# Loading part of w2 as two transfers, for 119 and for 9 partitions, in a one-token attention and gated feed-forward kernel

## The chip, the cores and the metric

The kernel runs on one core of a Trainium2 chip. The metric is device time in microseconds for one execution, here the median of several. A core has a matrix engine (TensorE, PE in the profile, with its weight loads as PEld), VectorE (DVE), ScalarE (ACT), GpSimd (POOL) and SyncE (SP), which here only issues transfers. Sixteen DMA engines move data between the device memory and the on-chip memory of 128 partitions.

## The reference, cut to what matters

One token is decoded. An attention over a cache of 32,768 positions with 32 query heads on 8 key/value heads, and a gated feed-forward branch, are mixed by a gate.

```python
q = (x @ wq).reshape(...)                     # x: (1, 1, 512), wq: (512, 4096)
scores = einsum("bhqd,bhkd->bhqk", q, k) * Dh ** -0.5
o = softmax(scores) @ v                       # k_cache, v_cache: (1, 8, 32768, 128)
a = o.reshape(...) @ wo                       # wo: (4096, 512)
gate = einsum("bsd,df->bsf", x, w1)           # w1, w3: (512, 1792)
up = einsum("bsd,df->bsf", x, w3)
b = einsum("bsf,fd->bsd", silu(gate) * up, w2)  # w2: (1792, 512)
g = sigmoid((x * gate_w).sum(-1))
out = g * a + (1 - g) * b
```

All of it is float32.

## The kernel before

The caches are cut into 32 units, four for each of the eight key/value heads. A unit is one block of keys (k0 to k31) and one of values (v0 to v31), each a transfer of 4 MB in which every partition receives 32 KB. All large loads go through `load` (line 69 issues them) on SyncE's queue and land in a pool named `stream` with four buffers, so a load can be issued as soon as the buffer four loads earlier has been read to its end.

The main loop runs over `UNITS + LAG` steps with `LAG = 5`: step i loads k of unit i and v of unit i - 5, transposes the keys on DVE in four chunks and multiplies them by the queries (lines 181 and 188), and multiplies the probabilities of an earlier unit by its values (`values`, line 277). The softmax of a head, and what follows its values, is cut into small steps which `defer` puts into a list and `tick` runs a fixed number of ticks later; this fixes the order of the instructions on each engine by hand. The feed-forward's w1 and w3 come in steps 2 and 3, and the hidden row is spread over partitions early (`htp`). In the last five steps no keys are left; v27 to v31 are loaded and used.

After the loop stands what the change touches. w2 (1792 x 512) is held as 14 row blocks: partition p has the rows 14p to 14p + 13, 2 KB each, 28 KB contiguous in device memory. The tile `w2t` (line 392) takes the stream buffer that v28 had, so its transfers (line 395) are issued when v28's matmuls are done. Three transfers bring blocks 0 to 7, 8 to 11 and 12 to 13, each for all 128 partitions. They stand in SyncE's queue behind v29, wo of the last head, v30 and v31. The last thing SyncE issues is the output (line 415).

On PE the order after the matmuls of v31 (line 277, tile o) is: heads of the last unit (po, line 289, which waits for ACT's copy ob, line 283), the first eight blocks of w2 (`ff_down(0, 8)`, tile pb, line 401, four matmuls a block), the product with wo (pa, line 303), the other six blocks of w2. DVE then adds pa to `acc`, scales it by the gate, and combines it with pb into `res` (line 414), which goes out.

Of the kernel before, what the change touches and what calls it, by code (L numbers as in the profile page):

```python
# [14 lines left out]
P = 128  # L15
# [4 lines left out]
def kernel(  # L20
# [13 lines left out]
    nc = tc.nc  # L34
# [29 lines left out]
    def misc(name):  # L64
        return ps_m.tile([P, 512], F32, tag="misc", name=name)
# [325 lines left out]

    w2t = stream.tile([P, FR, D], F32, tag="stream", name="w2")
    w2d = w2.rearrange("(p k) e -> p k e", k=FR)
    for a, b in ((0, 8), (8, 12), (12, 14)):
        nc.sync.dma_start(w2t[:, a:b, :], w2d[:, a:b, :])
    pb = misc("pb")

    def ff_down(a, b):
# [45 lines left out]
```

## Time and profile before

| | us |
|---|---|
| median of 3 runs | 705.38 (705.27 to 705.67) |
| the profiled execution | 705.64 |
| its span, first to last instruction | 703.9 |
| PE busy | 449.4 (64%) |
| PE weight loads busy | 161.6 (23%) |
| DVE busy | 317.6 (45%) |
| ACT busy | 69.3 (10%) |
| TensorE clock granted, mean | 0.735 |
| moved by DMA | 296.65 MB, mean 421 GB/s |

The span is what the profiler sees from the first to the last instruction of one execution; the time of that execution is 1.7 us longer. All numbers in the views come from this one execution. A view of lines or groups gives busy time and the mean of one instruction; the chain that ended last is followed back from the last instruction, each time to what released it. In the views of stretches, each engine has its busy time and its count of instructions in brackets, then come the clock granted to TensorE as a share of the full one, the mean busy share of the 16 DMA engines, and what they moved. A transfer's time "to landing" runs from its issue to the moment when its last part has arrived; a transfer that waits in the queue behind others has that wait in it.

### The profile page before, as it was taken

How to read it: one execution, taken by the hardware profiler on the slowest of the kernel's cores; microseconds unless marked ns; L12 is line 12 of the kernel's file. 1: busy time of each engine (PE TensorE's matmuls, PEld its weight loads, DVE VectorE, ACT ScalarE, POOL GpSimd, SP SyncE). 2: the span in 40 equal slices, each digit the busy share in tenths (PEclk: the TensorE clock that was granted, in tenths of full speed). 3: DMA queues.
4: the chain of work that ended last, by engine and by line, in shares of the span. 5: the costliest groups of instructions: out<-in, count | busy, mean ns of one | idle time of the engine just before them, and what ended most of it. 6: DMA issues, size and time to landing. Idle time of an engine off the chain costs nothing.

```text
span 703.9 us, 6780 instructions
## 1 busy us (share of the span) xinstructions
PE 449.4 (64%) x3014; PEld 161.6 (23%) x3014; DVE 317.6 (45%) x237; ACT 69.3 (10%) x175; POOL 1.6 (0%) x12
## 2 busy tenths in 40 slices
PE   2666578776863496545863679535966568547666
PEld 0331143114210042112320143102320142103213
DVE  1079556654752444554642455542643546523000
ACT  0100101210200002000120003000020002000100
POOL 0000000000000000000000000000000000000000
PEclk9766856695676759776676657967596757868868
DMA  8999999999999999999999999999999999999994
GB/s 369 435 435 426 435 429 399 427 429 434 427 426 431 436 427 432 423 427 434 427 428 431 434 426 435 424 428 434 429 433 417 437 426 435 420 436 430 423 428 198
DMA packets 14772, 296.65 MB, mean 421 GB/s; under 512 B 1556, under 2 KB 1560, under 8 KB 5784
## 3 DMA queue, kind: packets, MB, share of 16 engines
q1 hardware_dynamic: 14600, 296.23, 98.5%
q8 instruction: 23, 0.38, 0.2%
q14 instruction: 5, 0.04, 0.0%
q10 hardware_dynamic: 144, 0.00, 0.0%
HBM read 296.23 MB, written 0.00 MB: 421 GB/s over the span
## 4 chain that ended last, share of the span: by engine, by line
DMA 61%; PE 18%; DVE 14%; issue 6%; ACT 0%; SPq 0%; DVEq 0%
DMA k<-in_A_k_cache_dram 48%; DVE kt L181 12%; DMA v<-in_A_v_cache_dram 10%; PE pf L204 7%; PE s L188 4%; DMA wq<-in_A_wq_dram 3%; PE o L277 2%; PE pt L159 2%; DVE mx L213 1%; PE pw L320 1%; PE pq L142 1%; PE ph L350 1%; PE pb L401 0%; DVE rp L154 0%; DVE rep L345 0%
## 5 line engine op out<-in xcount | busy, mean ns | idle before, releaser
L181 DVE STREAM_TRANSPOSE kt<-k 128x2048 f32<-128x2048 f32 x128 | 288.9, 2290 | 225.7 <-DMA k<-in_A_k_cache_dram 219.7
L188 PE MATMUL s<-kt,win 128*32 128x512 f32 x1024 | 201.3, 872 | 209.1 <-DVE kt L181 168.4
L277 PE MATMUL o<-v,prob 128*32 128x512 f32 x1024 | 135.6, 677 | 15.1 <-DMA v<-in_A_v_cache_dram 15.1
L188 PEld LDWEIGHTS s<-kt,win 128*32 128x32 f32 x1024 | 25.7, 128 | 328.3 <-issue 181.0
L195 ACT COPY sb<-s 128x512 f32<-128x512 f32 x32 | 35.4, 1106 | 480.0 <-PE s L188 480.0
L277 PEld LDWEIGHTS o<-v,prob 128*32 128x32 f32 x1024 | 34.3, 124 | 105.3 <-issue 77.6
L204 PEld LDWEIGHTS pf<-pick,sb 128*128 128x128 f32 x256 | 52.5, 313 | 24.1 <-issue 24.1
L204 PE MATMUL pf<-pick,sb 128*128 128x64 f32 x256 | 55.3, 406 | 0.0
L213 DVE TENSOR_REDUCE mx<-pf 128x4 f32<-128x512 f32 x16 | 11.1, 692 | 49.6 <-PE pf L204 49.6
L245 ACT ACTIVATE prob<-pf,nm 128x128 f32<-128x128 f32 x64 | 23.4, 498 | 36.3 <-DVE nm L241 36.3
L296 DVE TENSOR_TENSOR otp<-po,recip 128x4 f32<-128x4 f32 x8 | 1.3, 167 | 51.4 <-PE po L289 51.4
L142 PE MATMUL pq<-wq,xp 128*32 128x512 f32 x64 | 10.6, 824 | 17.9 <-DMA wq<-in_A_wq_dram 17.9
L245 ACT ACTIVATION_READ_ACCUMULATOR prob<-pf,nm 128x1 f32 x64 | 14.8, 232 | 0.0
L154 DVE COPY rp<-qs 128x512 f32<-128x512 f32 x8 | 2.8, 415 | 24.5 <-ACT qs L148 24.5
L159 PE MATMUL pt<-ident,rp 128*128 128x4 f32 x64 | 11.3, 313 | 1.7 <-DVE rp L154 1.7
L159 PEld LDWEIGHTS pt<-ident,rp 128*128 128x128 f32 x64 | 11.2, 275 | 3.5 <-issue 3.5
L283 ACT COPY ob<-o 128x512 f32<-128x512 f32 x8 | 4.7, 587 | 73.5 <-PE o L277 73.5
L303 PE MATMUL pa<-wo,otp 128*32 128x128 f32 x256 | 11.8, 343 | 0.0
L303 PEld LDWEIGHTS pa<-wo,otp 128*32 128x32 f32 x256 | 10.1, 143 | 6.3 <-issue 6.0
L289 PEld LDWEIGHTS po<-fold,ob 128*128 128x128 f32 x64 | 7.7, 191 | 8.3 <-ACT ob L283 8.3
L289 PE MATMUL po<-fold,ob 128*128 128x4 f32 x64 | 8.4, 255 | 1.4 <-ACT ob L283 1.4
L142 PEld LDWEIGHTS pq<-wq,xp 128*32 128x32 f32 x64 | 2.6, 142 | 25.0 <-issue 19.8
(52 smaller groups left out, 71.8 us busy)
## 6 DMA issues: line engine op xcount, KB each, us to landing
k<-in_A_k_cache_dram SPq DMA_DIRECT2D x32, 4096.0 KB, 30.0
v<-in_A_v_cache_dram SPq DMA_DIRECT2D x32, 4096.0 KB, 34.8
wq<-in_A_wq_dram SPq DMA_DIRECT2D x2, 4096.0 KB, 16.9
wo<-in_A_wo_dram SPq DMA_DIRECT2D x8, 1024.0 KB, 27.4
w<-in_B_w_dram SPq DMA_DIRECT2D x2, 3584.0 KB, 33.8
w<-in_B_w_dram SPq DMA_DIRECT2D x1, 2048.0 KB, 30.2
w<-in_B_w_dram SPq DMA_DIRECT2D x1, 1024.0 KB, 32.3
w<-in_B_w_dram SPq DMA_DIRECT2D x1, 512.0 KB, 33.1
```

The lines of the kernel that those rows point to most:

```text
L142: nc.tensor.matmul(pq[b][32 * j:32 * j + 32, :], xp[:, c, :], wq_t[c // 2][:, o:o + REP * DH], start=(c == 0), stop=(c == NC - 1),)
L159: nc.tensor.matmul(pt[:, 4 * a:4 * a + 4], rp[:, a, :], sel, start=True, stop=True)
L181: nc.vector.transpose(kt.rearrange("p (n i) -> p n i", i=32), kin.rearrange("p (n c j) -> p c n j", c=4, j=32)[:, c],)
L188: nc.tensor.matmul(s_ps[0][32 * g:32 * g + 32, :], win[:, h, c, :], kt[:, 512 * g:512 * g + 512], start=(c == 0), stop=(c == 3),)
L195: nc.scalar.copy(sb[h][:, :, :, m], s_ps[0].rearrange("p (n i) -> p n i", i=32))
L204: nc.tensor.matmul(pf[h, f][:, 64 * a:64 * a + 64], sb[h][:, 8 * f + a].rearrange("p i m -> p (i m)"), pick, start=True, stop=True,)
L213: nc.vector.tensor_reduce(mx[:, f, :], pf[h, f].rearrange("p (n q) -> p q n", q=REP), axis=AX.X, op=ALU.max)
L245: nc.scalar.activation(prob[h % 2][:, 0:1024].rearrange("p (a n q) -> p a n q", a=16, q=REP)[:, :, 8 * f:8 * f + 8, q], pf[h, f].rearrange ...
L277: nc.tensor.matmul(o_ps[0][32 * t:32 * t + 32, :], prob[h % 2][:, o:o + 32], vt[:, n * P:(n + 4) * P], start=(r == 0 and g == 0), stop=(r ...
L289: nc.tensor.matmul(po[:, 0:REP], ob[:, b * P:(b + 1) * P], fold[:, 4 * b:4 * b + 4], start=(b == 0), stop=(b == 3),)
L303: nc.tensor.matmul(pa[32 * j:32 * j + 32, 0:P], otp[h % 2][:, q, :], wo_t[h][:, q, j * P:(j + 1) * P], start=(q == 0), stop=(q == REP - 1),)
L320: nc.tensor.matmul(p[32 * j:32 * j + 32, 0:FJ], xp[:, c, :], ff[name][:, o:o + FJ], start=(c == 0), stop=(c == NC - 1),)
```

## The change

The transfer of blocks 0 to 7 is cut. Blocks 0 to 2 are loaded by two transfers, one for partitions 0 to 118 and one for partitions 119 to 127; blocks 3 to 7 have a transfer of their own for all partitions. The two later transfers, the bytes moved and the matmuls stay as they are.

```diff
     w2t = stream.tile([P, FR, D], F32, tag="stream", name="w2")
     w2d = w2.rearrange("(p k) e -> p k e", k=FR)
-    for a, b in ((0, 8), (8, 12), (12, 14)):
-        nc.sync.dma_start(w2t[:, a:b, :], w2d[:, a:b, :])
+    for a, b, p0, p1 in ((0, 3, 0, 119), (0, 3, 119, P), (3, 8, 0, P), (8, 12, 0, P), (12, 14, 0, P)):
+        nc.sync.dma_start(w2t[p0:p1, a:b, :], w2d[p0:p1, a:b, :])
     pb = misc("pb")
```

## The prediction

> **What bounds the kernel now.** I read the page first.
>
> ```profile
> span 703.9 us, 6780 instructions
> DMA  8999999999999999999999999999999999999994
> DMA 61%; PE 18%; DVE 14%; issue 6%; ACT 0%; SPq 0%; DVEq 0%
> ```
>
> The DMA engines are over 90% busy in nearly every slice and hold 61% of the chain that ended last: the kernel streams its caches. The diff touches only its last transfer, so the chain after 640 us comes next, in order of time (start, duration, what).
>
> ```profile
> 653.61 36.15 DMA v<-in_A_v_cache_dram
> 689.77 0.04 issue
> 689.81 5.15 PE o L277 x32
> 694.96 0.02 issue
> 694.98 0.59 ACT ob L283
> 695.57 0.04 issue
> 695.62 1.05 PE po L289 x8
> 696.67 1.88 PE pb L401 x64
> 698.56 0.87 PE pa L303 x32
> 699.43 1.35 PE pb L401 x48
> 700.78 0.03 issue
> 700.81 0.35 DVE res L414
> ```
>
> The last block of values, v31, lands at 689.77. Behind it PE, ACT and DVE need eleven microseconds. w2 stands nowhere on this chain: both pb pieces follow PE's own earlier work. When does w2 land? The issues of its three transfers, then the page's times from issue to landing:
>
> ```profile
> 664.43 1.28 SPq L395 DMA_DIRECT2D w<-in_B_w_dram  x3
> ...
> L395 SPq DMA_DIRECT2D w<-in_B_w_dram x3: 328/424/425, 664.4 to 665.3; - x3
> ...
> w<-in_B_w_dram SPq DMA_DIRECT2D x1, 2048.0 KB, 30.2
> w<-in_B_w_dram SPq DMA_DIRECT2D x1, 1024.0 KB, 32.3
> w<-in_B_w_dram SPq DMA_DIRECT2D x1, 512.0 KB, 33.1
> ```
>
> Blocks 0 to 7 land at 664.43 + 30.2 = 694.6 and are read from 696.6; blocks 12 and 13 land at 665.3 + 33.1 = 698.4. They are needed after 32 of the 48 matmuls that start at 699.25 (below), about 0.026 us each, so at 700.1. w2 has 1.7 us to spare at its end and 2.0 at its start.
>
> One more view decides the case: the stretches around the end, with PE's busy time, granted clock (PEclk), the DMA share and GB/s at the right.
>
> ```profile
> 691.50:692.50 1.00, 1.00 (x12) 0.32 (x8) 0.00 (x0) 0.00 (x0) 0.00 (x0) 0.50 0.99 410
> 692.50:693.50 1.00, 1.00 (x16) 0.25 (x12) 0.00 (x0) 0.00 (x0) 0.00 (x0) 0.85 0.56 233
> 693.50:694.50 1.00, 1.00 (x16) 0.18 (x8) 0.00 (x0) 0.00 (x0) 0.00 (x0) 1.00 0.57 238
> 694.50:695.50 1.00, 0.40 (x4) 0.00 (x0) 0.00 (x0) 0.52 (x1) 0.00 (x0) 1.00 0.56 233
> 695.50:696.50 1.00, 0.88 (x8) 0.88 (x8) 0.00 (x0) 0.07 (x1) 0.00 (x0) 1.00 0.36 147
> 697.50:698.50 1.00, 1.00 (x47) 1.00 (x43) 0.00 (x0) 0.00 (x0) 0.00 (x0) 1.00 0.08 25
> ```
>
> The share falls in one step, 0.99 to 0.56, and stays there: 0.44 x 16 = 7 engines have run dry at 692.5, nine go on, the last until 698.4. So the sixteen engines are up to six microseconds apart, and what "v31 has landed" means is set by the latest of the nine.
>
> **The change, part by part.** Blocks 0 to 2 (6,144 bytes a partition) leave the first transfer and become two: partitions 0 to 118 and 119 to 127. Blocks 3 to 7 become the third.
>
> *Issue and waits.* Two more issues at 0.33 to 0.43 us each put the last one some 0.9 us later, near 666.2. It is hidden by 24 us of queue in front of w2; without that cover it would cost 0.9. Behind them SyncE has only the output's issue at 701.19. PE gets up to two more waits; the one that shows beside the first pb costs 51 ns, while PE waits for ACT's ob anyway.
>
> ```profile
> L401 PEldq EVENT_SEMAPHORE  x1: 51/51/51, 695.6 to 695.6; - x1
> ```
>
> *Who carries the 119 rows.* No transfer before has a number of rows that sixteen does not divide, except the output's four. A 4 MB block takes 9.74 us between the landings of v30 and v31 (starts 680.07 and 689.81 below), 262,144 bytes an engine, or 26.9 GB/s; one 6,144-byte row is 0.228 us. Bounds: spread over sixteen, 8 rows to an engine at most, 0 us more; all on one engine, 119 x 0.228 = 27.1 us. 119 is 7 x 17, so in equal shares it is seven engines with 17 rows, 3.9 us instead of 1.8; nine rows in equal shares go to nine engines. I take seven: the flat share before 691.5 says that 128 rows are dealt in equal shares, and seven is the most that 119 allows. Those seven then have 18 rows for 8, 2.3 us more; the engines left out have 8 rows, 1.8 us, less.
>
> [...]
>
> *Which seven.* The trace does not name engines. I take it that they are the seven early ones, since all nine late ones form a group apart (0.56, flat for three rows); the other case is a rival. The early seven have 14 blocks, 229,376 bytes, 8.5 us each, so they reach w2 at 692.5 - 8.5 = 684.0. That is 5.8 us before v31 has landed.
>
> *What those rows meet.* [...] Is 26.9 GB/s the engine's limit, or that of the way into its partitions? The rows cannot say: with nine engines and then one or two active the last one still needed 698.4 - 694.6 = 3.8 us for six blocks (98,304 bytes, 26 GB/s), so it is not the sum of all that limits, but it was alone on its partitions. Lower bound, the engine limits: v31 is not delayed, 0 us. Upper bound, the way limits: each gets 119/16 = 7.4 of these rows, at most 8, 1.7 to 1.8 us. If rows share, the seven need up to 2 x 3.9 = 7.8 us, of which 5.8 us, three quarters, come before v31's end: 1.3 us. The rows do not decide between the ends. I take 1.4 us, from the shared case: every rate seen had each engine on partitions of its own, and 26.9 GB/s came out alike in full and in thin traffic, which a narrow way into the partitions explains without more; the other end keeps a chance of its own.
>
> [...]
>
> *What 1.4 us on v31 costs.* Here the clock comes in.
>
> ```profile
> 680.07 6.54 PE L277 MATMUL o<-v,prob 128*32 128x512 f32 x32 [7.03 <-DMA v<-in_A_v_cache_dram]
> 689.81 5.09 PE L277 MATMUL o<-v,prob 128*32 128x512 f32 x32 [3.20 <-DMA v<-in_A_v_cache_dram]
> 699.25 1.49 PE L401 MATMUL pb<-w,htp 128*32 128x128 f32 x48
> ...
> 679.13:682.54 3.41, 2.47 (x12) 0.60 (x16) 0.00 (x0) 0.00 (x0) 0.00 (x0) 0.50 0.96 413
> 682.54:685.96 3.42, 3.42 (x20) 0.79 (x16) 0.00 (x0) 0.00 (x0) 0.00 (x0) 0.50 0.97 417
> 685.96:689.38 3.42, 0.65 (x8) 0.00 (x0) 0.00 (x0) 0.00 (x0) 0.00 (x0) 1.00 0.97 414
> 689.38:692.79 3.41, 2.98 (x16) 0.80 (x20) 0.00 (x0) 0.00 (x0) 0.00 (x0) 0.50 0.91 383
> 692.79:696.20 3.41, 2.69 (x26) 0.94 (x18) 0.00 (x0) 0.59 (x1) 0.00 (x0) 1.00 0.54 223
> ```
>
> The same 32 matmuls took 6.54 us for v30 and 5.09 for v31. At half clock one microsecond does half a microsecond's work: v30 had 5.89 at half and 0.65 at full (3.60 of work), v31 2.98 at half and 2.11 at full (3.60 again). The clock changes on a grid of 3.41 us. A stretch with 2.98 us of matmuls was followed by full clock, one with 2.47 by another half one. If v31 starts at 689.81 + 1.4 = 691.21, only 1.58 us of 689.38 to 692.79 are busy, the half clock lasts to 696.20, and the group ends at 696.20 + 3.60 - (696.20 - 691.21)/2 = 697.30 instead of 694.90: +2.4. For delays of 0.9 and 1.8 us the same line gives 2.15 and 2.6; under about 0.5 us it may stay near 0.2. All that follows, from ob to the output, is shifted by it unchanged.
>
> *Next late?* w2 is not: the seven finish by 684.0 + 7.8 + 0.2 + 11 blocks of 0.61 (6.7) = 698.7, the nine by 689.8 + 1.4 + 0.2 + 6.7 = 698.1, both before 700.1 + 2.4.
>
> **Sum:** issue 0, waits under 0.1, taken as 0, matmuls of v31 +2.4. The profiled execution would go from 705.64 (703.9 of span and 1.7 around it) to 708.0; it lies 0.26 above the median, so 705.38 + 2.4 = 707.8 us.
>
> **Rivals.**
>
> *No shared way* (the other side: not slower). The engines limit, v31 lands as before, the nine finish w2 1.8 us earlier, at 696.6, and nobody had waited: 705.4. For it: the rates fit an engine's limit as well. Against: nothing but the choice of bound above. It decides as soon as v31's delay is zero.
>
> *Shared, but the clock's grid falls otherwise,* or the delay is under 0.5 us: the delay enters alone or halved, +0.2 to +1.3, 706.1.
>
> *Late engines among the seven.* The latest then finishes w2 2.3 us later: 698.4 + 2.3 = 700.7 against 700.1, +0.6 (706.0). With a shared way its 17 rows take up to 3.9 more, 704.6, +4.5 (709.9); I put it at 708.5. The flat 0.56 speaks for a fixed group of nine, but not for which.
>
> *The rows are not bunched:* sixteen carry 7 or 8 rows each, nothing changes, 705.4. Or all 119 on one: 684.0 + 27.1 + 6.9 = 718.0 against 700.1, 723.3.
>
> *Faster.* In unprofiled executions the late engines might lag further and w2 set the end; 1.8 us less on the nine would then give up to -1.8, 703.6. Against: 1.7 us of slack, and 705.64 beside 705.38.
>
> **Chances.** Forecast 0.56; grid or small delay 0.08; no shared way 0.18; late among the seven 0.10 (0.08 of it shared); sixteen 0.03; one 0.02; faster 0.03. A measurement here tells 0.2%, 1.4 us, from no change. Slower: 0.56 + 0.08 + 0.02 = 0.66; within: 0.08 + 0.18 + 0.02 + 0.03 = 0.31; faster 0.03. The range takes in the unchanged time and most of the shared case with late engines: 705.2 to 709.2.
>
> **What would show it.** Right: v31's landing near 691.2 with the same issue time, a half-clock stretch after 692.8, an o group of about 6.1 us, the DMA share still near 1 after 692.5, and no wait of PE for w2. Wrong: v31 at 689.8 again (no sharing), PE waiting for w2 before pb (late engines among the seven), or the first transfer's landing far beyond 700 (one engine).

## The result, and the profile after

The changed kernel takes 711.78 us (median of 4, 711.01 to 712.41) beside 705.52 us (median of 4, 705.27 to 705.89) for the kernel before: a ratio of 1.0087 with a 95% interval of 1.0075 to 1.0100, 6.3 us slower. That is outside the predicted range of 705.2 to 709.2. The sign was right, the size was not.

The page of the changed kernel, from its profiled execution (712.20 us):

```profile
span 710.4 us, 6783 instructions
DMA 62%; PE 17%; DVE 14%; issue 6%; SPq 0%; ACT 0%; DVEq 0%
```

The chain that ended last, after 640 us, in order of time:

```profile
666.89 39.61 DMA w<-in_B_w_dram
706.51 0.04 issue
706.55 0.69 PE pb L401 x16
707.24 0.03 issue
707.26 0.35 DVE res L414
```

Before, this chain ran through v31, its matmuls, ob, po, pb and pa, and w2 stood nowhere on it. Now w2's last transfer stands between its issue at 666.89 and PE's last 16 matmuls, and landed at 706.51; before, it landed at 698.4.

PE's last groups (start, duration, group, in brackets the idle time before them and what ended it):

```profile
679.27 6.06 PE L277 MATMUL o<-v,prob 128*32 128x512 f32 x32 [7.02 <-DMA v<-in_A_v_cache_dram]
692.87 6.09 PE L277 MATMUL o<-v,prob 128*32 128x512 f32 x32 [7.53 <-DMA v<-in_A_v_cache_dram]
700.66 0.86 PE L401 MATMUL pb<-w,htp 128*32 128x128 f32 x24
702.82 1.30 PE L401 MATMUL pb<-w,htp 128*32 128x128 f32 x40 [1.30 <-DMA w<-in_B_w_dram]
705.30 1.08 PE L401 MATMUL pb<-w,htp 128*32 128x128 f32 x32 [0.31 <-DMA w<-in_B_w_dram]
706.55 0.64 PE L401 MATMUL pb<-w,htp 128*32 128x128 f32 x16 [0.17 <-DMA w<-in_B_w_dram]
```

The stream of this execution is 0.80 us ahead of the one before: v30's matmuls start at 679.27 instead of 680.07. From v30 to v31 it then takes 13.60 us instead of 9.74. So v31 is 3.86 us late. Behind it PE waits for w2 three times, 1.30 + 0.31 + 0.17 = 1.78 us, where it never waited before.

The stretches around v31's landing, of before and then of after (DMA share and GB/s at the right):

```profile
684.00:688.00 4.00, 2.61 (x16) 0.40 (x8) 0.00 (x0) 0.00 (x0) 0.00 (x0) 0.75 0.96 410
688.00:692.00 4.00, 2.19 (x12) 0.60 (x16) 0.00 (x0) 0.00 (x0) 0.00 (x0) 0.67 0.98 412
```

```profile
680.00:684.00 4.00, 4.00 (x24) 0.98 (x20) 0.00 (x0) 0.00 (x0) 0.00 (x0) 0.50 0.98 391
684.00:688.00 4.00, 1.33 (x12) 0.12 (x4) 0.00 (x0) 0.00 (x0) 0.00 (x0) 0.93 1.02 244
688.00:692.00 4.00, 0.00 (x0) 0.00 (x0) 0.00 (x0) 0.00 (x0) 0.00 (x0) 0.50 0.89 202
692.00:696.00 4.00, 3.13 (x16) 0.79 (x20) 0.00 (x0) 0.00 (x0) 0.00 (x0) 0.50 0.99 240
```

This is the finding to explain. From 684 on the sixteen engines are as busy as ever (share 0.89 to 1.02) and move little more than half as much. Each packet takes longer: in the trace v31's packets of 32,768 bytes took 1.21 to 1.23 us before, and after the change those that start from 684 on took 1.97 to 2.57 us. So here the busy share does not tell a moving engine from a held one (0.98 with 412 GB/s before, 0.89 with 202 after); only the GB/s beside it does.

The trace also has the completion signals of each transfer, sixteen for 128 rows. I take one signal for one engine's part: before the change seven of the sixteen signals of w2's last transfer came by 693.57 and nine from 695.95 on, and the DMA share from 692.5 to 695.5 is 0.56, nine sixteenths. For v31, us from the span's start:

```text
before  684.16 684.22 684.27 684.44 684.62 684.96 684.97 | 687.35 ... 689.77  (9)
after   684.09 684.12 684.23 684.46 684.59 685.28 685.65 | 689.90 ... 692.82  (9)
```

Seven early and nine late engines, as the falling DMA share had told. The first w2 transfer of the changed kernel has seven signals of its own, at 691.46, 691.63, 692.75, 692.79 and then at 698.71, 698.90 and 699.71; the second has nine. So 119 rows do run on seven engines and nine rows on nine, and three of the seven are late ones. I take it that the same three set w2's end: of the sixteen signals of its last transfer thirteen come by 701.70, and three at 705.78, 705.82 and 706.51, 6.8 to 7.1 us behind those three, where eleven blocks of 0.61 us take 6.7.

### The profile page after: what moved, and what is told of

It is laid out like the page before. It is cut to its first block, busy times and chain, and to the rows that moved or that the text cites. A ratio compares the mean times of both kernels' runs of the same rounds, so it can differ in the third digit from the quotient of the medians.

```text
span 710.4 us, 6783 instructions
## 1 busy us (share of the span) xinstructions
PE 448.0 (63%) x3014; PEld 157.8 (22%) x3014; DVE 317.3 (45%) x237; ACT 69.6 (10%) x175; POOL 1.7 (0%) x12
## 4 chain that ended last, share of the span: by engine, by line
DMA 62%; PE 17%; DVE 14%; issue 6%; SPq 0%; ACT 0%; DVEq 0%
DMA k<-in_A_k_cache_dram 49%; DVE kt L181 12%; PE pf L204 7%; DMA w<-in_B_w_dram 6%; PE s L188 5%; DMA v<-in_A_v_cache_dram 4%; DMA wq<-in_A_wq_dram 3%; PE pt L159 1%; PE o L277 1%; PE pq L142 1%; DVE mx L213 1%; PE ph L350 1%; PE pw L320 1%; DVE rep L345 0%; DVE win L167 0%
## 5 line engine op out<-in xcount | busy, mean ns | idle before, releaser
L277 PE MATMUL o<-v,prob 128*32 128x512 f32 x1024 | 133.2, 667 | 17.9 <-DMA v<-in_A_v_cache_dram 17.9
L142 PE MATMUL pq<-wq,xp 128*32 128x512 f32 x64 | 12.7, 964 | 16.9 <-DMA wq<-in_A_wq_dram 16.9
L303 PE MATMUL pa<-wo,otp 128*32 128x128 f32 x256 | 10.2, 309 | 0.0
L159 PEld LDWEIGHTS pt<-ident,rp 128*128 128x128 f32 x64 | 9.3, 233 | 3.9 <-issue 3.9
L159 PE MATMUL pt<-ident,rp 128*128 128x4 f32 x64 | 9.4, 283 | 1.1 <-DVE rp L154 1.1
## 6 DMA issues: line engine op xcount, KB each, us to landing
v<-in_A_v_cache_dram SPq DMA_DIRECT2D x32, 4096.0 KB, 34.9
```

What stands on the lines that cost most here:

```text
L142: nc.tensor.matmul(pq[b][32 * j:32 * j + 32, :], xp[:, c, :], wq_t[c // 2][:, o:o + REP * DH], start=(c == 0), stop=(c == NC - 1),)
L159: nc.tensor.matmul(pt[:, 4 * a:4 * a + 4], rp[:, a, :], sel, start=True, stop=True)
L277: nc.tensor.matmul(o_ps[0][32 * t:32 * t + 32, :], prob[h % 2][:, o:o + 32], vt[:, n * P:(n + 4) * P], start=(r == 0 and g == 0), stop=(r ...
L303: nc.tensor.matmul(pa[32 * j:32 * j + 32, 0:P], otp[h % 2][:, q, :], wo_t[h][:, q, j * P:(j + 1) * P], start=(q == 0), stop=(q == REP - 1),)
```

## The experiments

Two questions were open: why v31 is 3.9 us late when its own transfer was not touched, and why w2 ends so late. In the table, "v31 late" is the time between the starts of v30's and v31's matmuls less the 9.74 us of before; "v31's packets" is the time of one packet of 32,768 bytes that starts after 685 us; "waits for w2" is PE's idle time ahead of pb. These three come from the profiled execution, the ratio from repeated runs.

| kernel | ratio to before (95%) | v31 late | v31's packets | waits for w2 |
|---|---|---|---|---|
| changed kernel (first blocks, 119 + 9) | 1.0087 (1.0075 to 1.0100) | 3.86 | 2.00 to 2.57 | 1.78 |
| e2, first blocks, all 128 | 0.9993 (0.9983 to 1.0003) | -0.01 | 1.21 to 1.22 | 0 |
| e3, first blocks, 112 + 16 | 1.0052 (1.0037 to 1.0067) | 3.39 | 1.55 to 2.20 | 0 |
| e11, first blocks, 64 + 64 | 1.0059 (1.0043 to 1.0076) | 4.03 | 1.81 to 2.26 | 0 |
| e8, block 0 alone, 119 + 9 | 1.0029 (1.0016 to 1.0042) | 1.64 | 1.45 to 1.84 | 0 |
| e4, last blocks, 119 + 9 | 1.0036 (1.0024 to 1.0049) | -0.01 | 1.21 to 1.22 | 1.59 |
| e7, last blocks, 112 + 16 | 1.0011 (1.0001 to 1.0021) | -0.02 | 1.21 to 1.22 | 1.30 |
| e10, w2 as before, v31 in four parts | 1.0003 (0.9993 to 1.0014) | | | 2.15 |

**e2, the cut without uneven partitions.** In the diffs of e2, e3 and e4 a minus marks the line of the changed kernel.

```diff
-    for a, b, p0, p1 in ((0, 3, 0, 119), (0, 3, 119, P), (3, 8, 0, P), ...
+    for a, b, p0, p1 in ((0, 3, 0, P), (3, 8, 0, P), ...
```

> Blocks 0 to 2 in a transfer of their own, but for all 128 partitions; the rest as after the change. If the partitions' ways or the unequal shares are the cause, this is the time of before, 705.5 us within 0.2%, v31 lands on its old place and the stretch from 684 to 692 keeps 410 GB/s. If shorter rows (6,144 and 10,240 bytes in place of 16,384) or one more transfer were the cause, it is slower by several us like the changed kernel.

Its chain has v31 on its old place, and its stretch has the old rate:

```profile
653.10 36.13 DMA v<-in_A_v_cache_dram
...
684.00:688.00 4.00, 0.78 (x8) 0.00 (x0) 0.00 (x0) 0.00 (x0) 0.00 (x0) 1.00 0.95 402
```

No difference from before (0.9993). Rows of 6,144 and 10,240 bytes in place of 16,384 and one more transfer cost nothing here; it is the cut by partitions.

**e3, equal shares.**

```diff
-    ... ((0, 3, 0, 119), (0, 3, 119, P), ...
+    ... ((0, 3, 0, 112), (0, 3, 112, P), ...
```

> The same cut of blocks 0 to 2, at partition 112 instead of 119: 112 and 16 rows, both multiples of sixteen, so the shares of the engines can be equal (7 and 1 rows), but an engine's rows are not the eight partitions that it has in a full transfer. Ways into the partitions: slower by 2 us or more, with v31 late and the rate down between 684 and 692. Unequal shares: within 0.2% of before, 705.5.

```profile
652.94 39.82 DMA v<-in_A_v_cache_dram
692.76 0.04 issue
692.81 6.49 PE o L277 x32
...
684.00:688.00 4.00, 1.86 (x16) 0.29 (x8) 0.00 (x0) 0.00 (x0) 0.00 (x0) 0.90 1.03 256
```

v31 is nearly as late as in the changed kernel, although both transfers have sixteen signals, so that in equal shares every engine has 7 + 1 rows as it had 8. So the delay of v31 does not come from unequal shares. The bytes, their place in device memory and the size of a row are those of e2; what is left is that a row can go to another engine than in a full transfer. Rows for partitions that another engine writes in a 128-row transfer are called rows on foreign partitions below. PE does not wait for w2 here, whose last signal comes at 702.60: that second part of the loss is missing.

**e11, halves.** The same with `(0, 3, 0, 64), (0, 3, 64, P)`.

> Blocks 0 to 2 cut in halves, partitions 0 to 63 and 64 to 127: shares are equal (4 rows for each of sixteen engines in each transfer). If foreign partitions are the cause, v31 is late by 2 to 3.5 us as with the cut at 112, and the time 2 to 4 us above before. If it was the odd cut at 112 or 119, and halves keep each engine on its own partitions, no change within 0.2%.

```profile
680.21 6.26 PE L277 MATMUL o<-v,prob 128*32 128x512 f32 x32 [7.00 <-DMA v<-in_A_v_cache_dram]
693.98 6.20 PE L277 MATMUL o<-v,prob 128*32 128x512 f32 x32 [7.51 <-DMA v<-in_A_v_cache_dram]
```

v31 is 4.03 us late, the kernel 0.6% slower. Even the tidiest cut by partitions costs as much as the odd one at 112.

**e4 and e7, the cut behind v31.** The first blocks stay whole, and the last three (11 to 13) are cut.

```diff
-    ... ((0, 3, 0, 119), (0, 3, 119, P), (3, 8, 0, P), (8, 12, 0, P), (12, 14, 0, P)):
+    ... ((0, 8, 0, P), (8, 11, 0, P), (11, 14, 0, 119), (11, 14, 119, P)):
```

> The cut at 119 partitions moves from the first three blocks to the last three (11 to 13); blocks 0 to 7 and 8 to 10 have full transfers ahead of them. Both theories: v31 lands as before (the early engines come to the cut rows only at 684.1 + 6.8 = 690.9, after it), and the loss is that of w2's end alone. With only unequal shares the last block lands 2.3 us later than before, 0.6 us of it on PE: 706.1. With shared ways as strong as in the changed kernel (rows at half the rate) it lands 4 to 6 us later: 708 to 710, still 2 us or more below the changed kernel's 711.8.

> The cut at partition 112 (equal shares) in the last three blocks, where v31 has landed before the cut rows begin. If the loss has two parts, v31 late through shared ways and w2's end late because the seven that carry 17 rows include late engines, this version has neither and stands within 1 us of before (705.9 in the runs so far; 705.5 to 706.9). If shared ways alone make w2's end late too, it is 1.5 to 2.5 us slower, like the cut at 119 in the last blocks (+2.5).

PE in e4:

```profile
689.16 5.34 PE L277 MATMUL o<-v,prob 128*32 128x512 f32 x32 [4.17 <-DMA v<-in_A_v_cache_dram]
...
701.26 0.86 PE L401 MATMUL pb<-w,htp 128*32 128x128 f32 x24 [1.59 <-DMA w<-in_B_w_dram]
```

v31 is on time in both (-0.01 and -0.02), so here the rows must be in flight before v31 has landed to delay it. What remains is w2's end: +0.36% with 119 and +0.11% with 112 rows. The +0.36% are 2.5 us, at the low end of what was expected with shared ways, and well above the 0.6 of unequal shares alone. The two profiled executions look alike (waits of 1.59 and 1.30); that 119 costs more than 112 rests on the repeated runs, whose intervals do not overlap (e4's profiled execution was its fastest, 707.09 beside a median of 708.09). At the first blocks the same two cuts differ by 1.0087 against 1.0052, some 2.5 us. So seven engines with 17 rows cost about 2 us more than sixteen with 7, at either place.

**e8, a third of the bytes.** Block 0 alone is cut at 119, blocks 1 to 7 are one transfer.

> The cut at 119 partitions for block 0 alone (2,048 bytes a row, a third of the bytes), blocks 1 to 7 in one transfer. If both parts of the loss go with the bytes, a third of 6.3: v31 late by 1.2 to 1.4 us and, as w2's end has slack, 1.5 to 3 us in all. If a cut costs something fixed (a switch of partitions, a wait), nearly as slow as three blocks, 5 to 6 us.

+0.29% for a third of the bytes, a third of the loss. v31 is 1.64 us late, where a third of 3.86 is 1.29; so most of the price goes with the bytes, and a fixed part, if there is one, is about half a microsecond.

**e5, which engines are late.** The kernel before, with small transfers behind w2:

```diff
+    nc.sync.dma_start(few[0][0:1], k_cache[0, 0, 0:1])
+    nc.sync.dma_start(few[1][0:2], k_cache[0, 0, 0:2])
...
+    nc.sync.dma_start(few[4][0:9], k_cache[0, 0, 0:9])
```

> The kernel before, with five small transfers of 1, 2, 3, 5 and 9 rows of 512 bytes behind w2 in the same queue, into tiles that nothing reads. If a transfer of n rows, n up to 9, runs on the first n engines, each lands when the latest of these n engines has worked off w2. Prediction's step (the seven of the 119 rows are the early ones): the transfers of 1, 2, 3 and 5 rows land within a microsecond of each other, near 693 to 694, well before w2's last block at 698.4. Rival (late engines are among the seven): at least one of the transfers of 1 to 5 rows lands between 696 and 698.6.

The completion signals, from the trace:

```text
w2's last transfer   692.95 ... 693.89 (7)   696.05 ... 698.18 (9)
1 row    693.24
2 rows   693.41 693.94
3 rows   693.46 693.59 694.10
5 rows   693.64 693.77 694.07 694.28 696.23
9 rows   693.12 693.43 693.82 693.95 694.26 694.46 696.41 696.49 698.13
```

A transfer of n rows gives n signals. The sets grow: with one, two and three rows all carriers are early; of the next two one is late; among the first nine there are three late ones, the very latest (698.1) among them. The changed kernel's seven signals for 119 rows, four early and three late, agree. The rival is right in this: the seven that carry 17 rows include late engines.

**e1, each transfer alone.** The computation is left out; eleven loads, each issued when the one before has landed:

> Only transfers are left of the kernel, one after the other, each issued when the one before has landed: from the key cache, with 32,768 bytes a row, 128, 119, 112, 64, 32, 16 and 17 partitions; from w2, with 6,144 bytes a row, 128, 119, 112 and 9. The whole computation is left out. Engine as the limit: 128 rows 9.7 us plus some fixed time, 119 rows on seven engines 17 x 1.216 = 20.7, 112 rows 8.5, 64 rows 4.9, 32 rows 2.4, 16 rows 1.2, 17 rows 20.7 if one engine has them all. Way into the partitions as the limit: 128 rows the same, 16 rows four times as long (4.9), 64 rows as long as 128 or nearly, 119 rows up to 41, 112 rows up to 17. For w2: 119 rows 3.9 by the first, up to 8 by the second.

The chain of waits shows all of them one by one (from the issue to the landing): of the key cache 128, 119, 112, 64, 32, 16 and 17 rows, then of w2 128, 119, 112 and 9 rows:

```profile
0.73 12.00 DMA t<-in_A_k_cache_dram
...
12.75 30.97 DMA t<-in_A_k_cache_dram
...
43.74 16.19 DMA t<-in_A_k_cache_dram
...
59.95 12.51 DMA t<-in_A_k_cache_dram
...
72.47 7.04 DMA t<-in_A_k_cache_dram
...
79.53 6.73 DMA t<-in_A_k_cache_dram
...
86.28 22.47 DMA t<-in_A_k_cache_dram
...
108.76 4.05 DMA t<-in_B_w_dram
...
112.83 7.20 DMA t<-in_B_w_dram
...
120.04 4.32 DMA t<-in_B_w_dram
...
124.38 2.13 DMA t<-in_B_w_dram
```

128 rows take 9.74 us in the stream, so about 2.3 us are fixed. Without them 64 rows take 10.2 us, more than 128; 32 and 16 rows 4.8 and 4.5, where an engine's own pace would give 2.4 and 1.2. That is near what was expected if the way into the partitions is the limit (4.9 us for 16 rows, 64 rows as long as 128). As rates, without the 2.3 us: 16 rows came in at 117 GB/s, 32 at 219, 64 at 205, 128 at 431; in units of the 26.9 GB/s of one engine in the stream that is an estimate of 4, 8, 8 and 16. So 16 rows for 16 neighbouring partitions, a transfer of sixteen signals in e3, came in at the pace of four engines. More than these rates no run shows of the ways. 17 rows take 20.2, 17 times 1.19, at 10 to 30 GB/s with a DMA share under 0.1 in the slices between: one engine, and 27.6 GB/s for it alone. 112 and 119 rows take 13.9 and 28.7, between the engine's pace (8.5 and 20.7) and twice that, the upper ends of the expectation (17 and 41).

**e6, beside a full block.** The computation is left out; a 128-row block of keys on SyncE's queue, and at the same moment 6,144-byte rows of w2 on ScalarE's.

> Only transfers: a 128-row block of keys (32,768 bytes a row) on SyncE's queue, five times, each after the one before; the first alone, beside the others at the same moment a transfer of 6,144 bytes a row from w2 on ScalarE's queue, with 128, 112, 119 and 64 rows. The whole computation is left out. Alone the block takes 12.0 us. If rows on foreign partitions cost only their bytes, the block beside any of them takes 12.0 to 14 us (128 rows are 1.8 us more of each engine's time, 112 and 119 the same bytes or less, 119 up to 16 as seven engines have 17 rows, 3.9 us, each). If they hinder more than their bytes, the block beside 112 rows takes clearly longer than beside 128: 15 us or more.

The end of each pair, beside 128, 112, 119 and 64 rows:

```profile
13.02 13.93 DMA small<-in_B_w_dram
...
27.21 15.55 DMA big<-in_A_k_cache_dram
...
43.09 18.81 DMA small<-in_B_w_dram
...
62.16 13.85 DMA big<-in_A_k_cache_dram
```

112 rows beside the block cost 15.55 - 12.00 = 3.5 us, 128 rows with more bytes 1.9. The 112 rows are 7 for each engine, 7 x 0.228 = 1.6 us; so they cost about twice their bytes. The 64 rows cost as much as 128, 1.9 us, which e1's 205 GB/s for 64 rows would explain by bytes alone (393,216 bytes in 1.9 us); it is the 112 rows that bytes do not explain.

**e9, one engine on foreign partitions.** The computation is left out.

```diff
+    nc.sync.dma_start(big, kd[0, 1])
+    nc.scalar.dma_start(small[64:81], w2d[64:81])
...
+    nc.sync.dma_start(big, kd[0, 3])
+    nc.scalar.dma_start(small[0:16], w2d[16:32])
```

> Only transfers: a 128-row block of keys on SyncE's queue four times, one after the other; beside the second, at the same moment on ScalarE's queue, 17 rows of 28,672 bytes for partitions 64 to 80, beside the third 17 rows for partitions 0 to 16, beside the fourth 16 rows for partitions 0 to 15. The whole computation is left out. 17 rows run on one engine (20.2 us alone). If an engine on foreign partitions hinders only those whose partitions it writes, most of the sixteen parts of the second and third block land as alone, 12.0 us after the issue, and only the parts of the four or five engines whose partitions are written are late, by up to 4 us, beside that of the one engine that carries both. If every engine is slowed (a common way), all sixteen parts are late by several us. With 16 rows on 16 engines for partitions 0 to 15, every engine has one row for a crowded way: all parts late by 4 us or more by both.

Completion signals of the 128-row block, us after its issue:

```text
beside 17 rows (64 to 80)   11.59 ... 12.00 (14)   15.85   24.76
beside 16 rows (0 to 15)    16.05 ... 16.61 (16)
```

One engine on foreign partitions left fourteen of sixteen alone. Only four of its 17 rows had been started when those fourteen landed; the fifteenth part is late by about these four rows (4 x 1.07 = 4.3 us), the sixteenth, at 24.76, I take for that of the engine which carries the rows. (Beside 17 rows for partitions 0 to 16, of which five had been started by then, fifteen of sixteen parts landed within 12.6 us; whose partitions those five rows wrote, the trace does not say.) With one row for partitions 0 to 15 on each engine all sixteen are some 4.5 us late. As expected by both readings, this does not tell them apart: with sixteen rows on sixteen engines each has one of these rows itself.

**e12, the end of the kernel by itself.** The computation is left out; four sets in one queue: nine rows that make nine engines late, a block, then w2's rows for 128, 112, 119 and 64 partitions.

> Only transfers, four times the same three in one queue: 9 rows of 98,304 bytes, which make nine engines late by 3.7 us, a 128-row block of keys, then rows of 28,672 bytes from w2 with 128, 112, 119 and 64 partitions; each set after the one before. The whole computation is left out. It is the end of the kernel by itself: seven early engines, nine late ones, and behind the block a transfer that deals its rows otherwise. [...] If all engines slow down as soon as some write foreign partitions, all nine late parts are 2 us or more later beside 112 and beside 64.

Completion signals of the block, us after the set's first issue:

```text
then 128 rows   22.25 ... 22.33 (7)   24.98 ... 25.89 (9)
then 112 rows   22.22 ... 22.34 (7)   27.33 ... 28.19 (8)   30.16
then 119 rows   22.17 ... 22.26 (7)   25.32 ... 25.79 (9)
then  64 rows   22.43 ... 22.57 (7)   31.55 ... 32.74 (9)
```

The block is the same each time; only what follows it in the queue differs. With 112 rows behind it all nine late parts lose 2.3 us or more, with 64 rows 6.6 us or more. All nine were slowed alike: with 64 rows behind, the last two packets of each took 3.59 to 3.69 us, with 128 rows 1.21 to 1.22. If each of the seven early engines writes one row at a time, seven such rows are under way; had a packet been slowed only by one for its own way, some of the nine should have kept their pace.

Of those 64 rows the seven early engines carry 28, 28 x 1.07 = 30 us at an engine's pace; the nine late parts together lose 9 x 6.6 = 59 us, twice that. With 119 rows they lose nothing: here, if the sets grow as in e5, the seven that carry them are among the late nine, and no early engine writes foreign partitions.

The first set shows the same by chance. Its nine rows go to nine neighbouring partitions (in e1 16 rows for 16 neighbouring partitions came in at 117 GB/s), and while they were under way the seven other engines hardly got on with the block. The first three packets of each took 3.75 to 4.88 us, and the seven parts landed 22.3 us after the set's first issue, where a block alone takes 12.0 (columns: us, DVE and POOL busy, clock, DMA share, GB/s):

```profile
2.00:6.00 4.00, 0.00 (x0) 0.00 (x0) 1.00 0.50 70
6.00:10.00 4.00, 0.00 (x0) 0.00 (x0) 1.00 1.55 168
10.00:14.00 4.00, 0.00 (x0) 0.00 (x0) 1.00 0.51 66
14.00:18.00 4.00, 0.00 (x0) 0.00 (x0) 1.00 0.75 262
18.00:22.00 4.00, 0.00 (x0) 0.00 (x0) 1.00 0.97 418
```

The view counts a packet where it starts, hence the share of 1.55; only the three rows from 2 to 14 us together say what moved, (70 + 168 + 66)/3 = 101 GB/s. Seven free engines at 26.9 GB/s each would have moved 188 GB/s alone; here all sixteen together moved 101. The block's rows are for all 128 partitions, and all of the seven were slowed; I read it as traffic to few partitions slowing traffic that does not go there. Which partitions the seven were writing, and which engines share a path, the trace does not say.

**e10, v31 in four parts,** since its 5 us of matmuls stood at the end of the chain:

```diff
-                vt = load(f"v{v}", NB * DH, vd[v])
+                for g in range(4):
+                    nc.sync.dma_start(vt[:, 2048 * g:2048 * g + 2048], vd[v][:, 2048 * g:2048 * g + 2048])
```

> w2 as before the change; v31 comes in four transfers of 8,192 bytes a row for all 128 partitions, one for each group of its matmuls. v31's last part lands where the whole one did (689.8), but three quarters of its matmuls are done by then, so that 1 to 1.7 us of them are left instead of 5.1. Then w2's last landing (698.4) sets the end: 698.4 + 0.7 of matmuls + 0.4 + 0.35 is 699.9 for DVE's end instead of 701.2, and the time 1.2 to 1.8 us less than before, 0.2%. If the matmuls of v31 were not what held the end, no change.

```profile
689.66 1.07 PE L277 MATMUL o<-v,prob 128*32 128x512 f32 x8 [0.80 <-DMA v<-in_A_v_cache_dram]
691.43 1.05 PE L289 MATMUL po<-fold,ob 128*128 128x4 f32 x8 [0.70 <-ACT ob L283]
694.64 3.64 PE L406 MATMUL pb<-w,htp 128*32 128x128 f32 x64 [2.15 <-DMA w<-in_B_w_dram]
```

v31 is done 4 us earlier, and nothing is won, where 1.2 to 1.8 us had been expected: PE then waits 2.15 us for w2 and does the first 64 of its matmuls at about half clock (0.56 in 692 to 696, 0.59 in 696 to 700), in 3.64 us instead of 1.95. No version beat the kernel before.

## Why the prediction was wrong

**Issues and waits:** right. Five issues started from 664.6 to 666.9, the last when v29 had landed (0.7 us later than the prediction had it), and nobody waited for them.

**Who carries the rows:** right. Seven and nine signals. In e5 1, 2, 3, 5 and 9 rows gave as many signals.

**Which seven:** the first step that failed. "I take it that they are the seven early ones" was read out of one number, 7, that stood in two places: seven engines had run dry at 692.5, and seven carry the rows. They are not the same seven (e5): three are late. The rival "late engines among the seven" had it, put at 708.5 with a chance of 0.10; even its upper figure, 709.9, lies below the 711.78 measured, since it counted the 17 rows of a late engine but no delay of v31 in front of them.

**What those rows meet:** right in kind, wrong in size, and this is the larger failure. The term "1.4 us on v31" measured 3.86, above its own upper bound of 1.8. The bound counted bytes: 7.4 rows of 0.228 us on each of sixteen ways. No run shows that number of ways, nor the term of 1.4 us, two rows that halve each other's pace; the runs show v31 3.39 to 4.03 us late with three blocks cut (after, e3, e11), and in e1 117 GB/s into 16 partitions. In e9 a count of bytes fits a single engine on foreign partitions. With several, in the changed kernel, all engines together slowed to some 55% (244 and 202 GB/s for 410 and 412), v31's packets from 684 on take 2.0 to 2.6 us instead of 1.2, and in e12 the late parts lose twice what the bytes take. The reasoning saw that the limit was not the sum of all traffic, from a stretch in which one or two engines were still active (26 GB/s), and took it for a rule.

**The clock:** the rule was right, the exact agreement is luck. In the traces of before and after the granted clock is full or half, in stretches that are multiples of 3.41 us. Half clock lasted until 697.85 in this execution:

```profile
696.00:697.00 1.00, 1.00 (x8) 0.20 (x4) 0.00 (x0) 0.00 (x0) 0.00 (x0) 0.50 0.77 287
697.00:698.00 1.00, 1.00 (x12) 0.27 (x8) 0.00 (x0) 0.00 (x0) 0.00 (x0) 0.57 0.85 227
698.00:699.00 1.00, 0.96 (x12) 0.05 (x4) 0.00 (x0) 0.00 (x0) 0.00 (x0) 1.00 0.75 227
```

(0.57 of full clock in 697 to 698 is half until about 697.86.) The line of the prediction then gives 697.85 + 3.60 - (697.85 - 692.87)/2 = 698.96 for the end of v31's matmuls; they ended at 692.87 + 6.09 = 698.96. But the grid of this execution lies 1.65 us later than that of before (697.85 against 696.20). On the old grid the same line gives 696.20 + 3.60 - (696.20 - 692.87)/2 = 698.14 for this start, a length of 5.27 and +0.2 instead of +1.0. In the other kernels with a late v31 the group took 6.20 to 6.60 us (e3, e8, e11), in those where v31 was on time 5.34 (e2, e4, e7): the clock adds about a microsecond, though not the same one each time.

**"w2 is not" late next:** wrong, as a consequence of the two steps. The late ones of the seven began their 17 rows at about 690 to 693 and ended them at 698.7 to 699.7, and w2's last block landed at 706.5 instead of 698.4. The prediction had the nine engines end at 698.1 and the seven at 698.7.

**The sum.** DVE's last instruction starts at 707.26 instead of 700.81, 6.45 later:

| term | predicted | measured |
|---|---|---|
| start of v31's matmuls | +1.4 | 692.87 - 689.81 = +3.06 (3.86 late, stream 0.80 ahead) |
| their length | +1.0 | 6.09 - 5.09 = +1.00 |
| from their end to DVE's last start | 0 | (707.26 - 698.96) - (700.81 - 694.90) = +2.39 |

The repeated runs, +6.3, agree. Of it e3 and e11, which have the delay of v31 and the clock but not the seven engines, account for 0.52% and 0.59%, 3.7 and 4.2 us; the rest, 2.1 to 2.6 us, is a difference between kernels, and the three late signals of w2's last transfer say where it comes from: the late engines among the seven.

**What stays open.** Why crowding costs more than its bytes is shown in e6 and e12 only by its effect. Which rows of a transfer an engine gets, cut or whole, is not in the trace, so it is not known whose ways were crowded in the kernel itself. That it is the partitions written that crowd, and not the places read in device memory, is argued from e2 and e3, which read the same bytes, and from the pace of e1; no run kept the partitions and changed what is read.

## What to carry to other kernels

In this kernel a load for fewer than all 128 partitions was a different kind of transfer, not a smaller one: 119 rows ran on seven engines, and while such rows were under way, what stood ahead of them in the queue on the late engines was slowed too (v31's packets 1.97 to 2.57 us instead of 1.21 to 1.23). Where a kernel is like this one, cut a large load along the free dimension (e2: 0.9993), not by partitions (e3, e11: 0.5 to 0.6%). Read GB/s beside the DMA share, since engines that moved half as much counted as busy here (share 0.89 at 202 GB/s); and when two counts in a profile agree, test that they count the same things before a step rests on it.

## What the runs showed of the hardware that was not expected

- While nine engines wrote nine neighbouring partitions, packets of the seven others took 3.75 to 4.88 us instead of 1.22, and all sixteen moved about 101 GB/s (e12).
- With 64 rows behind a full block, the last packets of nine engines took three times their time, and all of them the same: 3.59 to 3.69 us (e12).
- A load of 64 rows alone takes longer than one of 128 (12.51 against 12.00 us, e1).
- The sixteen engines end up to 5.6 us apart (v31 before: 684.16 to 689.77) although in equal shares all have the same bytes. In the trace of before they begin within 0.6 us and then single engines fall back in steps of about 1.6 us, the first time when one 16 KB packet of instructions had been fetched at 34.9 us (fifteen parts of the next block at 42.0 to 42.5, one at 44.1); that these fetches are the cause was not tried.
